# Moving the late DMA issues of a fused GFNet and FFN training kernel from SyncE's queue to GpSimd's, and some copies from ScalarE to VectorE

## The chip, the cores and the metric

The kernel runs on one core of one Trainium2 chip. The metric is the device time of that core in microseconds (us) for one execution of the whole program, which is a single launch. The kernel before takes 437.01 us, the median of three runs (436.89 to 438.28).

A core has engines with an instruction stream each: TensorE (matmuls; PE in the profile, with PEld for its weight loads), VectorE (DVE), ScalarE (ACT), GpSimd (POOL) and SyncE (SP), which only issues DMA transfers here. Every engine runs its stream in order, and waits at an instruction until the semaphores that it needs have come. A DMA transfer is issued by an engine's instruction, and then carried out by the DMA engines of the core while the issuing engine goes on.

## What is computed

The reference is one transformer-like block and all its gradients. Cut to what matters:

```python
def _fwd_reference(A_x, A_w_r, A_w_i, B_x, B_w1, B_b1, B_w2, B_b2, c, w_mod):
    def _A_ref(x, w_r, w_i):                       # GFNet filter
        X = rfft2(x.astype(float32), axes=(-2, -1))
        X = X * (w_r + 1j * w_i)
        return irfft2(X, s=(S, D)).astype(bfloat16)
    def _B_ref(x, w1, b1, w2, b2):                 # FFN with squared ReLU
        h = einsum('bsd,df->bsf', x, w1) + b1
        r = where(h > 0, h, 0)
        return einsum('bsf,fd->bsd', r * r, w2) + b2
    mod = (silu(c) @ w_mod).reshape(1, 6, 1, -1)
    sa, ca, ga, sb, cb, gb = (mod[:, i] for i in range(6))
    h = layernorm(x) * (1 + ca) + sa
    x = x + ga * _A_ref(h, w_r, w_i)
    h = layernorm(x) * (1 + cb) + sb
    return x + gb * _B_ref(h, w1, b1, w2, b2)

def reference(...):
    out, vjp = jax.vjp(f, A_x, A_w_r, A_w_i, B_w1, B_b1, B_w2, B_b2, c, w_mod)
    return (out, *vjp(grad_out))
```

x and grad_out are 1 x 2048 x 512, the FFN is 1792 wide, w_r and w_i are 2048 x 257, w_mod is 512 x 3072; all are bf16. There are ten outputs: the block's output and nine gradients.

## The kernel before

The Fourier transforms are matmuls with constant matrices, done in steps: f1 along the row, f2 and f3 across rows (both in the function `spec_f23`), and g1, g2, g3 back. The program goes through these phases:

1. Layer norm of x and f1; beside it, in the free time of TensorE, `ga = gT @ w2T` for all of the FFN's width. Then `spec_f23` with the filter's multiplication, and g1.
2. Per block of 512 rows: g2, g3, second norm, hidden layer, output layer, and the gradient back through the FFN's rows.
3. The spectrum window: `spec_f23` of the gradient, the gradients of w_r and w_i, and between its steps the gradient of w1 (`grad_w1`) and parts of the gradient of w_mod (`GMod.emit`).
4. The last window: g1, g2, g3 of the gradient, the first norm backwards in pairs of 128-row tiles (`row_pair`), and between them the gradient of w2 (`grad_w2`).

The code is written with a scheduler: `high_priority`, `Priority(tc, LATE)` and `issue_after` move instructions within an engine's stream. A tile pool with `bufs=n` gives n buffers in turn, and a tile waits until the last use of its buffer is over.

Phase 1. The scaling of w2T by `2 gb`, one half on VectorE and one on ScalarE, and the copies of ga out of PSUM, a third on VectorE:

```python
def scale_w2(h):
    for dc in range(4):
        wh = w2T[:, dc, h * F2:(h + 1) * F2]
        if h == 0:
            nc.vector.tensor_scalar(wh, wh, gb2x[:, dc:dc + 1], None, op0=ALU.mult)
        else:
            nc.scalar.activation(wh, wh, AF.Copy, scale=gb2x[:, dc:dc + 1])

for q in range(4):
    ...                                  # bn_stats of 4 tiles of x_sb, the last is `stats`
    if q == 1:
        with tc.issue_after(stats.ins): scale_w2(0)
    ...                                  # x_sb normalized, the last on ScalarE is `scaled`
    if q == 1:
        with tc.issue_after(scaled.ins): scale_w2(1)
    ...                                  # f1 of these tiles
nc.sync.dma_start(n1_dram, x_sb)         # 2 MB: the normalized rows, for the last window
...
nc.sync.dma_start(LF_dram, K["LFall"])   # a constant, later loaded transposed as LG
with Priority(tc, LATE):
    for b in range(NB):                  # 4
        for fc in range(NFC):            # 14
            ps = mmps.tile([P, SB], FP32, name="mm")
            for dc in range(4): nc.tensor.matmul(ps, lhsT=w2T[...], rhs=gT[b][:, :, dc, :], ...)
            with tc.high_priority():
                if fc % 3 == 0: nc.vector.tensor_copy(out=gaT[b][:, fc, :], in_=ps)
                else:           nc.scalar.copy(out=gaT[b][:, fc, :], in_=ps)
```

`spec_f23`, used in phases 1 (with `dc`, a constant term) and 3 (with `dc` None). After each of its eight f2 steps two strided halves of AE are copied out of PSUM, both by ScalarE:

```python
def spec_f23(tc, K, UT, AEs, dc, dest, elementwise, after):
    ...
    for gi in range(8):
        ...                              # f2: matmuls into ps
        nc.scalar.activation(dst[0], src[:, 0], AF.Copy, scale=EF_S)
        nc.scalar.activation(dst[1], src[:, 1], AF.Copy, scale=EF_S)
        if gi > 0: f3(gi - 1)            # matmuls, a copy, then elementwise(gi), after(gi)
# phase 1: the spectrum X in tiles Xs (memset on GpSimd), stored; parts of LG loaded transposed
def ew_f(gi, X):
    cmul(...)
    nc.sync.dma_start(xs_dram[:, gi], X)
    if 2 <= gi < 6: lg_part(gi - 2)      # LG <- LF_dram with transpose, LG_dram <- LG
```

Phase 2, its loads. `x1` is the first block of rows of x, for the second norm; w1T is loaded with a transpose:

```python
load_rows(0)                             # x1 <- x, on SyncE
nc.sync.dma_start(w1, w1_view)
nc.sync.dma_start(w2, w2_view)
nc.sync.dma_start(w1T, B_w1, transpose=True)
```

Phase 3. The gradient of w1 in 16 units of 16 matmuls, each evacuated by ScalarE into half of a tile of two buffers that a store empties:

```python
def grad_w1(fb, dc):
    ...                                  # 16 matmuls into ps
    if fb % 2 == 0: w1o[0] = gwa.tile([P, 2, W4], BF16, name="gw1", bufs=2)
    nc.scalar.copy(out=w1o[0][:, fb % 2, :], in_=ps[:, 0:W4])
    if fb % 2 == 1: nc.sync.dma_start(out4_view[...], w1o[0]...)

class GMod: def emit(self, jc, q, row, pool, ppool):
    ...                                  # gmbc: one row broadcast by a matmul
    for dc in range(0, 4, 2):
        wmc = pool.tile([P, 2, D], BF16, name="wmc", bufs=self.bufs)     # 2, later 4
        nc.sync.dma_start(wmc, self.wm_view[:, dc:dc + 2, cs])
        gwm = pool.tile([P, 2, D], BF16, name="gwm", bufs=self.bufs)
        for i in range(2): ...           # gwm = gmbc * scf; gsc = sum of wmc * gmbc
        nc.sync.dma_start(self.out9_view[:, dc:dc + 2, cs], gwm)

def load(gi): ...                        # SyncE: LF[gi] (gi >= 4), Z[gi], Xb[gi]
def ew_b(gi, G):
    cmul(...); cmul(...)                 # Z[gi] in place, and gW, a tile of 3 buffers
    for i, o in enumerate((out_2, out_3)):
        for p0_, n, rows_ in w_parts(o, gi):
            nc.sync.dma_start(rows_, gW[p0_:p0_ + n, i, :, 0:DF])        # 34 stores in all
def after_b(gi):
    if gi + 4 < 8: load(gi + 4)
    ...
    fill_w1(2 if 0 < gi < 6 else 1)      # units of grad_w1 in between
    if gi % 2 == 1: gms.pop(0)()         # one GMod.emit
```

Phase 4. `load_hn` is a transposing load; the row loads of pair t + 4 are issued after pair t:

```python
def load_hn():
    if fc < NFC:
        hns.append(endp.get("hn", gwp).tile([P, NT, P], BF16, name="hn", bufs=4))
        nc.sync.dma_start(hns[fc], h_dram[fc, :, :], transpose=True)

def grad_w2(fc):
    ...                                  # 16 matmuls of hns[fc] with g_sb
    nc.vector.tensor_tensor(gw, ps, modb[:, GB_B, :], op=ALU.mult)
    nc.sync.dma_start(out6_view[:, fc, :], gw)
    load_hn()

def load_rows3(t):
    if t < NT:
        rows3[t] = (fin.tile([P, 2, D], BF16, name="n1"), fin.tile([P, 2, D], BF16, name="gxl"))   # 2 buffers each
        nc.sync.dma_start(rows3[t][0], n1_dram[:, t:t + 2, :])
        nc.sync.dma_start(rows3[t][1], gx1_dram[:, t:t + 2, :])

def row_pair(t, Ts):
    n1, gxl = rows3[t]
    ...                                  # g3, copies out of PSUM, unfold: gh1
    nc.vector.tensor_tensor(gn, gh1, ..., op=ALU.mult)
    ...                                  # ScalarE: gs = gn * inv1
    nc.vector.tensor_tensor(q1, gh1, n1, op=ALU.mult)                      # L1231, the first use of n1
    ...
    for i in range(2):                                                     # L1239, the last use of n1
        nc.vector.tensor_scalar(gn[:, i, :], n1[:, i, :], rr[:, i, 3:4], rr[:, i, 2:3], op0=ALU.mult, op1=ALU.add)
    nc.vector.tensor_tensor(gs, gn, gs, op=ALU.add)
    nc.vector.tensor_tensor(gx, gs, gxl, op=ALU.add)
    nc.sync.dma_start(out1_view[:, t:t + 2, :], gx)
    load_rows3(t + 4)

nc.sync.dma_start(g_sb, g_view)
load_hn(); load_rows3(0); load_rows3(2)
for _ in range(3): load_hn()
...                                      # g1
for t in range(0, NT, 2):                # 8 pairs, with grad_w2 (fill) between them
    fill(1); row_pair(t, Ts); Ts = g2_pair(t + 2); ...
...                                      # the last two GMod.emit, the rest of grad_w2,
nc.sync.dma_start(out_8..., gcr)         # and the gradient of c
```

Of the kernel before, what the change touches and what calls it, by code (L numbers as in the profile page):

```python
# [9 lines left out]
AF = mybir.ActivationFunctionType  # L10
# [9 lines left out]
DF = 257  # L20
# [273 lines left out]
def spec_f23(tc, K, UT, AEs, dc, dest, elementwise, after=lambda gi: None):  # L294

    nc = tc.nc
    with tc.tile_pool(name="psB", bufs=1, space=PSUM) as psB_pool, \
# [14 lines left out]
        for gi in range(8):  # L312
# [12 lines left out]
            nc.scalar.activation(dst[1], src[:, 1], AF.Copy, scale=EF_S)  # L325
# [113 lines left out]
class GMod:  # L439
# [7 lines left out]
    def emit(self, jc, q, row, pool, ppool):  # L447
# [8 lines left out]
        for dc in range(0, 4, 2):  # L456
            wmc = pool.tile([P, 2, D], BF16, name="wmc", bufs=self.bufs)
            nc.sync.dma_start(wmc, self.wm_view[:, dc:dc + 2, cs])
# [8 lines left out]
            nc.sync.dma_start(self.out9_view[:, dc:dc + 2, cs], gwm)  # L467
# [3 lines left out]
def kernel(  # L471
# [144 lines left out]
    def scale_w2(h):  # L616
        for dc in range(4):
            wh = w2T[:, dc, h * F2:(h + 1) * F2]
            if h == 0:
                nc.vector.tensor_scalar(wh, wh, gb2x[:, dc:dc + 1], None, op0=ALU.mult)  # L620
            else:
                nc.scalar.activation(wh, wh, AF.Copy, scale=gb2x[:, dc:dc + 1])

    for q in range(4):
# [6 lines left out]
        if q == 1:  # L633
            with tc.issue_after(stats.ins):
                scale_w2(0)
# [4 lines left out]
        for j in range(4):  # L640
            t = 4 * q + j
            if j == 0:
                nc.vector.tensor_scalar(x_sb[:, t, :], x_sb[:, t, :], inv1[:, t:t + 1], nb[:, j:j + 1], op0=ALU.mult, op1=ALU.add)
            else:
                scaled = nc.scalar.activation(x_sb[:, t, :], x_sb[:, t, :], AF.Identity, bias=nb[:, j:j + 1], scale=inv1[:, t:t + 1])
        if q == 1:
            with tc.issue_after(scaled.ins):
                scale_w2(1)
# [40 lines left out]
    with Priority(tc, LATE):  # L689
        for b in range(NB):  # L690
            for fc in range(NFC):
# [3 lines left out]
                with tc.high_priority():  # L695
                    if fc % 3 == 0:
# [342 lines left out]
    def grad_b1():  # L1039
# [8 lines left out]
        nc.sync.dma_start(out_5.rearrange("(q f) -> q f", q=NFB), b4[0:P:32, :])  # L1048

    def add_quadrants(ps, pool, out, scale=None):  # L1050
# [6 lines left out]
        def add():  # L1057
# [7 lines left out]
            nc.sync.dma_start(out, row)  # L1065
# [11 lines left out]
    def grad_w1(fb, dc):  # L1077
# [8 lines left out]
        if fb % 2 == 1:  # L1086
            nc.sync.dma_start(out4_view[:, dc, (fb - 1) * W4:(fb + 1) * W4], w1o[0].rearrange("p a f -> p (a f)"))
# [16 lines left out]
    with tc.tile_pool(name="f23b", bufs=2) as fr, tc.tile_pool(name="ewb", bufs=2) as ew:  # L1104
# [12 lines left out]
        def ew_b(gi, G):  # L1117
# [3 lines left out]
            for i, o in enumerate((out_2, out_3)):  # L1121
                for p0_, n, rows_ in w_parts(o, gi):
                    nc.sync.dma_start(rows_, gW[p0_:p0_ + n, i, :, 0:DF])
# [23 lines left out]
    def grad_w2(fc):  # L1147
# [6 lines left out]
        nc.sync.dma_start(out6_view[:, fc, :], gw)  # L1154
# [12 lines left out]
    def load_rows3(t):  # L1167
        if t < NT:
            rows3[t] = (fin.tile([P, 2, D], BF16, name="n1"), fin.tile([P, 2, D], BF16, name="gxl"))
            nc.sync.dma_start(rows3[t][0], n1_dram[:, t:t + 2, :])  # L1170
            nc.sync.dma_start(rows3[t][1], gx1_dram[:, t:t + 2, :])
# [33 lines left out]
    with tc.tile_pool(name="psE", bufs=2, space=PSUM) as psE, tc.tile_pool(name="psS1", bufs=1, space=PSUM) as psS1:  # L1205
# [11 lines left out]
        def row_pair(t, Ts):  # L1217
# [25 lines left out]
            nc.sync.dma_start(out1_view[:, t:t + 2, :], gx)  # L1243
# [36 lines left out]
        nc.sync.dma_start(out_8.rearrange("b (dc p) -> (b dc) p", p=P), gcr)  # L1280
# [42 lines left out]
```

## Time and profile before

| | |
|---|---|
| time, median of 3 runs | 437.01 us (436.89 to 438.28) |
| span of the profiled execution | 436.5 us |
| granted TensorE clock, mean | 0.992 |
| DMA packets, bytes | 149,138 of 149,738 packets and 100.12 of 101.09 MB on the hardware queue of SyncE |
| costliest matmul groups | L694 58.1, L853 53.6, L1150 51.6, L1081 51.5, L880 49.9 and 49.1 us |

The stages, by the trace: the first phase without its spectrum pass runs to 57 us, the forward spectrum pass to 82, g1 to 92, rows and second norm until the first hidden-layer matmul (L853) at 116.8, the blocks of the FFN to 285, the spectrum window to 351, and the last window to the end.

How to read the lines. "L1231" is line 1231 of the kernel. A row of a timeline gives the start in us, the time from start to end, the engine, the line, the operation, the tiles as out<-in with their shape, and how many instructions the row joins; at its end, in brackets, the idle time before it and what ended that. In "[3.12 <-DMA n<-n_dram]" the engine stood idle for 3.12 us until the transfer into tile n landed. "SPq" is SyncE as an issuer of DMA: its time is that of the issue, not of the transfer. A "releaser" is found from semaphore events, and where an instruction waits for several things, the last to come is named.

Tile names in the profile are the program's, sometimes those of a reader or of an alias: n is `n1`, gw is both the tile `gw1` of `grad_w1` and the tile `gw` of `grad_w2` (the line tells which), gab is a block of `gaT`, and x is `x1` after 90 us.

### The profile page before, as it was taken

How to read it: one execution, taken by the hardware profiler on the slowest of the kernel's cores; microseconds unless marked ns; L12 is line 12 of the kernel's file. 1: busy time of each engine (PE TensorE's matmuls, PEld its weight loads, DVE VectorE, ACT ScalarE, POOL GpSimd, SP SyncE). 2: the span in 40 equal slices, each digit the busy share in tenths (PEclk: the TensorE clock that was granted, in tenths of full speed). 3: DMA queues.
4: the chain of work that ended last, by engine and by line, in shares of the span. 5: the costliest groups of instructions: out<-in, count | busy, mean ns of one | idle time of the engine just before them, and what ended most of it. 6: DMA issues, size and time to landing. Idle time of an engine off the chain costs nothing.

```text
span 436.5 us, 7027 instructions
## 1 busy us (share of the span) xinstructions
PE 398.5 (91%) x2353; PEld 195.4 (45%) x2375; DVE 351.4 (80%) x846; ACT 261.2 (60%) x493; POOL 13.0 (3%) x64
## 2 busy tenths in 40 slices
PE   2789989999999999999999999999899799993996
PEld 0335446654444434443444444455455464441332
DVE  6887758959997588969897998909686968978896
ACT  5797889769881286348536765365348375445331
POOL 6120000000000000000000000000000000000000
PEclk9998999999999999999999999999999999999899
DMA  8995779999298469669965997987995699999984
GB/s 240 238 291 146 188 290 267 279 311 256 91 379 245 136 114 352 165 165 229 270 195 153 222 338 267 211 204 229 273 300 158 168 253 259 222 260 244 275 235 144
DMA packets 149738, 101.09 MB, mean 232 GB/s; under 512 B 98753, under 2 KB 135494, under 8 KB 149062
## 3 DMA queue, kind: packets, MB, share of 16 engines
q1 hardware_dynamic: 149138, 100.12, 86.6%
q10 hardware_dynamic: 564, 0.53, 0.4%
q8 instruction: 18, 0.29, 0.3%
q14 instruction: 18, 0.15, 0.1%
HBM read 35.44 MB, written 41.60 MB: 176 GB/s over the span
## 4 chain that ended last, share of the span: by engine, by line
PE 35%; DVE 28%; DMA 14%; ACT 12%; SPq 5%; issue 5%; POOL 1%; ACTq 0%; DVEq 0%
PE og L880 10%; PE mm L853 6%; PE mm L694 4%; PE mm L1150 4%; DMA n<-n_dram 3%; DMA out_dram<-gw 2%; DMA x<-in_A_x_dram 2%; DVE gm_junk L465 2%; PE psG L341 2%; SPq L1145 2%; PE mod_ps L595 2%; PE mm L1081 2%; DMA n_dram<-x_sb 2%; DVE l_st L795 1%; ACT r L855 1%
## 5 line engine op out<-in xcount | busy, mean ns | idle before, releaser
L694 PE MATMUL mm<-gT,w2T 128*128 128x512 bf16 x224 | 58.1, 383 | 3.4 <-DVE gab L697 2.7
L853 PE MATMUL mm<-h2T,w 128*128 128x512 bf16 x224 | 53.6, 379 | 1.7 <-ACT r L855 1.5
L1150 PE MATMUL mm<-g_sb,hn 128*128 128x512 bf16 x217 | 51.6, 387 | 3.8 <-DVE gw L1153 3.4
L1081 PE MATMUL mm<-gab,h_sb 128*128 128x448 bf16 x256 | 51.5, 352 | 2.5 <-ACT gw L1085 2.5
L880 PE MATMUL og<-w1T,gab 128*128 128x512 bf16 x218 | 49.9, 379 | 1.1 <-DVE o L945 0.8
L880 PE MATMUL og<-w,h 128*128 128x512 bf16 x217 | 49.1, 379 | 0.3
L855 ACT ACTIVATE r<-mm,b1col 128x512 bf16<-128x512 f32 x56 | 37.0, 684 | 6.1 <-PE mm L853 3.7
L1081 PEld LDWEIGHTS <-h_sb 128*128 128x128 bf16 x256 | 24.6, 98 | 24.2 <-issue 3.6
L853 PEld LDWEIGHTS <-w 128*128 128x128 bf16 x224 | 21.1, 97 | 30.6 <-issue 8.8
L1150 PEld LDWEIGHTS <-hn 128*128 128x128 bf16 x224 | 21.3, 99 | 29.8 <-issue 7.1
L880 PEld LDWEIGHTS <-h 128*128 128x128 bf16 x224 | 21.8, 98 | 26.1 <-issue 0.9
L880 PEld LDWEIGHTS <-gab 128*128 128x128 bf16 x224 | 21.6, 98 | 25.9 <-issue 1.4
L694 PEld LDWEIGHTS <-w2T 128*128 128x128 bf16 x224 | 20.9, 98 | 23.1 <-issue 6.5
L893 ACT CAST G<-og 128x512 bf16<-128x512 f32 x16 | 9.2, 580 | 27.9 <-PE og L880 27.9
L699 ACT CAST gab<-mm 128x512 bf16<-128x512 f32 x36 | 21.7, 602 | 3.0 <-PE mm L694 2.9
L857 DVE TENSOR_TENSOR h<-r 128x1024 bf16<-128x1024 bf16 x28 | 19.2, 687 | 4.8 <-ACT r L855 4.8
L1085 ACT CAST gw<-mm 128x448 bf16<-128x448 f32 x16 | 8.7, 543 | 24.0 <-DMA out_dram<-gw 15.0
L1230 ACT ACTIVATE gs<-gn,inv 128x512 bf16<-128x512 bf16 x16 | 11.4, 716 | 18.3 <-DVE gn L1228 18.3
L413 DVE TENSOR_TENSOR p<-Z,G 128x1028 bf16<-128x1028 bf16 x8 | 5.6, 697 | 19.9 <-DMA Xb<-xs_dram 11.6
L372 ACT ACTIVATE Tsb<-psT 128x512 bf16<-128x512 f32 x32 | 18.5, 604 | 1.6 <-PE psT L370 1.6
L465 DVE SCALAR_TENSOR_TENSOR gm_junk<-wmc,onef,gmbc 128x512 bf16<-128x512 bf16 x24 | 17.9, 747 | 1.9 <-DMA wmc<-in_w_mod_dram 1.0
L697 DVE CAST gab<-mm 128x512 bf16<-128x512 f32 x20 | 13.7, 686 | 6.8 <-PE mm L694 6.7
(287 smaller groups left out, 757.1 us busy)
## 6 DMA issues: line engine op xcount, KB each, us to landing
h_dram<-h SPq DMA_DIRECT2D x28, 256.0 KB, 3.6
gh_dram<-gab SPq DMA_DIRECT2D x28, 256.0 KB, 3.8
w<-in_B_w_dram SPq DMA_DIRECT2D x2, 1792.0 KB, 7.7
wmc<-in_w_mod_dram SPq DMA_DIRECT2D x12, 256.0 KB, 4.7
out_dram<-gwm SPq DMA_DIRECT2D x12, 256.0 KB, 3.7
wz_dram<-Z SPq DMA_DIRECT2D x8, 258.0 KB, 2.4
xs_dram<-Xs SPq DMA_DIRECT2D x8, 258.0 KB, 3.2
Z<-wz_dram SPq DMA_DIRECT2D x8, 258.0 KB, 4.3
```

Of the source, the lines that this page charges most:

```text
L372: nc.scalar.activation(Tsb, ps, AF.Copy, scale=EF_S)
L465: nc.vector.scalar_tensor_tensor(out=junk, in0=wmc[:, i, :], scalar=K["onef"], in1=gmbc, op0=ALU.mult, op1=ALU.mult, accum_out=self.gsc[:, ...
L694: nc.tensor.matmul(ps, lhsT=w2T[:, dc, fc * P:(fc + 1) * P], rhs=gT[b][:, :, dc, :], start=(dc == 0), stop=(dc == 3))
L697: nc.vector.tensor_copy(out=gaT[b][:, fc, :], in_=ps)
L699: nc.scalar.copy(out=gaT[b][:, fc, :], in_=ps)
L853: nc.tensor.matmul(ps, lhsT=w1[:, dc, (fc + i) * P:(fc + i + 1) * P], rhs=h2T[b][:, :, dc, :], start=(dc == 0), stop=(dc == 3))
L855: nc.scalar.activation(r[:, i, :], ps, AF.Relu, bias=b1col[:, fc + i:fc + i + 1])
L857: nc.vector.tensor_tensor(h2, r, r, op=ALU.mult)
L880: nc.tensor.matmul(ps, lhsT=lhs(fc), rhs=rhs[:, fc, :], start=(fc == 0), stop=(fc == NFC - 1))
L1081: nc.tensor.matmul(ps[:, 0:W4], lhsT=h2_sb[:, t, dc * P:(dc + 1) * P], rhs=ghn[t // 4][:, t % 4, fs], start=(t == 0), stop=(t == NT - 1))
L1150: nc.tensor.matmul(ps, lhsT=hns[fc][:, t, :], rhs=g_sb[:, t, :], start=(t == 0), stop=(t == NT - 1))
L1230: nc.scalar.activation(gs[:, i, :], gn[:, i, :], AF.Copy, scale=inv1[:, t + i:t + i + 1], accum_out=rr[:, i, 0:1])
```

## The change

In phases 3 and 4 all transfers were issued by SyncE, among them the transposing loads, in the order of the program. The change leaves the transposes and the loads of the spectrum with SyncE, and moves the rest to GpSimd, which has hardly any work after the first phase: the stores of the gradients of w1, w2, w_r, w_i, w_mod, x, b1, b2 and c, the loads of w_mod's blocks (wmc) and the row loads (n1, gxl). A store that waits for its data then holds up no load behind it on SyncE, and a row load doesn't wait for a transpose to be issued.

In phase 1 it shifts work from ScalarE to VectorE: the second of the two AE copies in the forward `spec_f23`, the half of w2's scaling that ScalarE did, and half instead of a third of the ga copies. The scaling of w2 is also placed earlier in the stream.

```diff
@@ spec_f23
             nc.scalar.activation(dst[0], src[:, 0], AF.Copy, scale=EF_S)
-            nc.scalar.activation(dst[1], src[:, 1], AF.Copy, scale=EF_S)
+            if dc is None:
+                nc.scalar.activation(dst[1], src[:, 1], AF.Copy, scale=EF_S)
+            else:
+                nc.vector.tensor_scalar(dst[1], src[:, 1], EF_S, None, op0=ALU.mult)
@@ GMod.emit
-            nc.sync.dma_start(wmc, self.wm_view[:, dc:dc + 2, cs])
+            nc.gpsimd.dma_start(wmc, self.wm_view[:, dc:dc + 2, cs])
 ...
-            nc.sync.dma_start(self.out9_view[:, dc:dc + 2, cs], gwm)
+            nc.gpsimd.dma_start(self.out9_view[:, dc:dc + 2, cs], gwm)
@@ scale_w2
-            if h == 0:
-                nc.vector.tensor_scalar(wh, wh, gb2x[:, dc:dc + 1], None, op0=ALU.mult)
-            else:
-                nc.scalar.activation(wh, wh, AF.Copy, scale=gb2x[:, dc:dc + 1])
+            nc.vector.tensor_scalar(wh, wh, gb2x[:, dc:dc + 1], None, op0=ALU.mult)
+
+    scale_w2(0)
 ...
         if q == 1:
             with tc.issue_after(stats.ins):
-                scale_w2(0)
+                scale_w2(1)
 ...
-        if q == 1:
-            with tc.issue_after(scaled.ins):
-                scale_w2(1)
@@ ga copies
-                    if fc % 3 == 0:
+                    if fc % 2 == 0:
                         nc.vector.tensor_copy(out=gaT[b][:, fc, :], in_=ps)
@@ grad_b1, add_quadrants, grad_w1, ew_b, grad_w2, load_rows3, row_pair, end
-        nc.sync.dma_start(out_5.rearrange("(q f) -> q f", q=NFB), b4[0:P:32, :])
+        nc.gpsimd.dma_start(out_5.rearrange("(q f) -> q f", q=NFB), b4[0:P:32, :])
 ...
-            nc.sync.dma_start(out, row)
+            nc.gpsimd.dma_start(out, row)
 ...
-            nc.sync.dma_start(out4_view[:, dc, (fb - 1) * W4:(fb + 1) * W4], ...)
+            nc.gpsimd.dma_start(out4_view[:, dc, (fb - 1) * W4:(fb + 1) * W4], ...)
 ...
-                    nc.sync.dma_start(rows_, gW[p0_:p0_ + n, i, :, 0:DF])
+                    nc.gpsimd.dma_start(rows_, gW[p0_:p0_ + n, i, :, 0:DF])
 ...
-        nc.sync.dma_start(out6_view[:, fc, :], gw)
+        nc.gpsimd.dma_start(out6_view[:, fc, :], gw)
 ...
-            nc.sync.dma_start(rows3[t][0], n1_dram[:, t:t + 2, :])
-            nc.sync.dma_start(rows3[t][1], gx1_dram[:, t:t + 2, :])
+            nc.gpsimd.dma_start(rows3[t][0], n1_dram[:, t:t + 2, :])
+            nc.gpsimd.dma_start(rows3[t][1], gx1_dram[:, t:t + 2, :])
 ...
-            nc.sync.dma_start(out1_view[:, t:t + 2, :], gx)
+            nc.gpsimd.dma_start(out1_view[:, t:t + 2, :], gx)
 ...
-        nc.sync.dma_start(out_8.rearrange("b (dc p) -> (b dc) p", p=P), gcr)
+        nc.gpsimd.dma_start(out_8.rearrange("b (dc p) -> (b dc) p", p=P), gcr)
```

That is 107 issues of 34 gW, 12 wmc, 12 gwm, 8 + 14 gw, 8 n1, 8 gxl, 8 gx and 3 small ones. The scheduler, given the new program, also orders some of SyncE's instructions anew: the load of x1 stands behind the transposing load of w1T where it stood ahead of it, and the store of the constant LF stands behind the last transpose of gT.

## The prediction

> **What bounds the kernel now.** I read the busy shares first, then cut the span into its stages by windows, then read the timelines of SyncE's DMA queue, VectorE, ScalarE and TensorE in each stage.
>
> ```profile
> PE 398.5 (91%) x2353; PEld 195.4 (45%) x2375; DVE 351.4 (80%) x846; ACT 261.2 (60%) x493; POOL 13.0 (3%) x64
> ```
>
> TensorE (PE) is busy 91% of 436.5 us, so at most some 38 us are idle, and VectorE (DVE) is next. GpSimd (POOL) is free. The windows by stage (columns: length, busy us and count of PE, PEld, DVE, ACT, POOL, then granted clock, DMA share, GB/s):
>
> ```profile
> 57.00:82.00 25.00, 22.24 (x168) 13.68 (x167) 18.24 (x45) 23.26 (x43) 0.67 (x9) 1.00 1.06 298
> 285.00:351.00 66.00, 60.74 (x470) 35.62 (x469) 45.90 (x108) 33.49 (x62) 0.00 (x0) 1.00 0.75 223
> 351.00:436.50 85.50, 74.15 (x412) 33.74 (x417) 69.89 (x171) 38.45 (x82) 0.00 (x0) 0.98 0.96 236
> ```
>
> Outside the first microseconds, most of the idle TensorE time that one can hope for lies in the last window: 11.3 us, against 5.3 us in the spectrum window (285 to 351). In the first spectrum pass (57 to 82) ScalarE is busy 93% of the time. Now the queue of SyncE in the last window, where a transposing load holds the queue while it is issued:
>
> ```profile
> 351.20 7.23 SPq L1145 DMA_TRANSPOSE hn<-h_dram  x1
> 358.48 1.26 SPq L1170 DMA_DIRECT2D n<-n_dram  x1
> ...
> 383.73 4.86 SPq L1145 DMA_TRANSPOSE hn<-h_dram  x2
> 388.68 0.53 SPq L1170 DMA_DIRECT2D n<-n_dram  x1
> ...
> 393.27 4.46 SPq L1145 DMA_TRANSPOSE hn<-h_dram  x1
> 397.83 0.52 SPq L1170 DMA_DIRECT2D n<-n_dram  x1
> ```
>
> Each row load n is issued the moment the transposes before it are through. VectorE then waits for it, and TensorE waits for VectorE:
>
> ```profile
> 392.68 0.69 DVE L1231 TENSOR_TENSOR q<-gh,n 128x1024 bf16<-128x1024 bf16 x1 [3.12 <-DMA n<-n_dram]
> 401.80 0.69 DVE L1231 TENSOR_TENSOR q<-gh,n 128x1024 bf16<-128x1024 bf16 x1 [1.38 <-DMA n<-n_dram]
> ```
> ```profile
> 397.96 0.38 PE L1060 MATMUL mm<-b,ones_col 128*1 128x512 bf16 x1 [3.48 <-DVE gn L1239]
> 403.15 1.86 PE L1150 MATMUL mm<-g_sb,hn 128*128 128x512 bf16 x4 [3.40 <-DVE gw L1153]
> ```
>
> Those two holes in TensorE also cost clock: the windows from 395 to 415 us show 0.91 and 0.92 where the neighbours show 1.00. In the spectrum window the pattern is another one: ScalarE waits for the store of a weight gradient to free one of two buffers.
>
> ```profile
> 311.92 0.53 ACT L1085 CAST gw<-mm 128x448 bf16<-128x448 f32 x1 [7.96 <-DMA out_dram<-gw]
> 328.09 0.53 ACT L1085 CAST gw<-mm 128x448 bf16<-128x448 f32 x1 [7.05 <-DMA out_dram<-gw]
> ```
>
> **What the Trainium skill says.** (1) "DMA: Bandwidth & Descriptors", section "Issuing engines are not separate DMA queues": all queues feed the same 16 engines, so a second issuing engine saves issue time alone, usually small. The trace agrees on plain copies (0.35 to 0.6 us an issue here), not on transposes: 7.23 and 4.86 us of issue stand ahead of the row loads above, and that is what a second queue saves. (2) The same page, "Latency and other measured facts": about 1 us to the first byte from GpSimd's queue, with descriptors written in software, against 0.6 us from SyncE's. No run here shows GpSimd issuing a DMA. (3) "SBUF — State Buffer", "Who interferes with whom": VectorE copies and tensor_scalar in two-port modes and GpSimd exclude each other, each for a whole instruction; tensor_tensor does not stop descriptor writing (the page calls this inferred). No trace here shows it; the exposed operations in the last window are L1239 (16 x 0.41 us) and L464.
>
> **The change part by part.**
>
> *Step 1, first phase, engine time.* ScalarE loses four w2 scalings (4 x 1.04 us), 8 of 36 gab copies (8 x 0.60) and 8 AE copies (8 x about 0.8): 4.2 + 4.8 + 6.4 = 15.4 us. VectorE takes them: 4 x 0.45 + 8 x 0.69 + 8 x 0.69 (an evacuation of 128x512 from PSUM costs it 0.69) = 12.8 us. In the instruction order of the changed kernel, 184 of the 224 mm matmuls stand ahead of the g1 stage, against 144 before: 40 x 0.215 us = 8.6 us of TensorE work is meant to be done earlier.
>
> *Step 2, what gates the first phase.* That is not worth 8.6 us. The Xs tiles wait for the 2 MB store of x_sb to be read out: GpSimd's memset of Xs waits 6.5 us and ScalarE starts at 64.97 us, after SyncE has worked through its Z loads until 57.4 us. Neither moves. Then LG follows: the LF store, issued at 61.05 and landed 10.7 us later, is put behind the last transpose of gT in the new order, which I put at +1 to +2 us; issuing the last two LG transposes back to back returns about 0.6 us. And the order of SyncE changes here:
>
> ```profile
> 91.72 0.33 SPq L763 DMA_DIRECT2D x<-in_A_x_dram  x1
> 92.10 13.61 SPq L983 DMA_TRANSPOSE w1T<-in_B_w_dram  x1
> ```
>
> In the changed program x stands behind w1T. It landed at 101.5 us; now I expect 105 to 108. From landing to the first hidden-layer matmul it took 15.3 us (to 116.8), with VectorE full; without 4 gab copies of 0.6 us inside that stretch, and with the unfolding done while waiting, I put it at 9 to 12 us. So the hidden layer begins at 114 to 120, middle 117.3: **+0.5 us**. The middle of the kernel, 117 to 285 us, keeps its TensorE order and moves with its start.
>
> *Step 3, spectrum window.* 107 DMA issues move to GpSimd in all (34 gW, 12 wmc, 12 gwm, 8 + 14 gw, 8 n, 8 gxl, 8 gx, 3 small). 58 fall between about 299 and 350 us. Their order is static: the first gw store comes after 6 gW stores, the second 10 entries later. If one costs GpSimd about 1 us (an estimate: the page's first-byte figure taken as issue cost), the first goes out at 299 + 6 = 305 rather than 307.5, the second at 315 rather than 310.4, and the third near 320 rather than 322. The first and third gate the 7.96 and 7.05 us waits, behind which TensorE loses only 1.7 and 0.8 us; the second could become a new gate. Of the 5.3 us of holes I count on **-2 us**.
>
> *Step 4, last window.* Row loads no longer stand behind transposes. n for the fifth pair can be issued once L1239 of the third pair has run, at 381.1, not 388.68; it lands (3.95 to 4.2 us) before 389.5, where VectorE began to wait. VectorE's waits there are 1.7 (first n), 3.1, 1.4, 1.1 and about 1.4 in smaller ones: 8.7 us. VectorE becomes the bound of this window; its order is unchanged. I take 7 of the 8.7 as gained: **-7 us**.
>
> *Step 5, tail.* The last four stores (two gwm, one gw, gcr) go one after another through GpSimd. At 1 us against SyncE's 0.3 to 0.6, and with a slower first byte, I add **+1.5 us**.
>
> Sum: +0.5 - 2 - 7 + 1.5 = -7, so 430. I keep 1.5 us back for tensor_scalar against GpSimd, a quarter of a microsecond at 6 of the 16 places. **Predicted: 431.5 us.**
>
> **The rivals.**
> (a) *GpSimd's queue becomes the bound.* For it: 58 issues in 51 us, full at 0.9 us each. At 1.4 us they would take 81 us, the second gw store would leave 14 us late, and the first row loads, which stand behind all of them, would not leave before about 370. Then step 3 turns to +8 or more and step 4 shrinks to -3: 443 to 448 us. Against it: nothing in this trace, as POOL issued no DMA.
> (b) *The queue is no limit and the engines take it.* If a GpSimd issue costs what SyncE's does (0.6 us), the spectrum window loses nearly all its holes (-5) and the row loads leave at about 348: 423 to 426 us.
> (c) *The transfers were bound by the DMA engines anyway.* The DMA share in 355 to 385 us is 1.06 to 1.12. If transposes and row loads share rather than queue, each lasts longer, hn comes late in place of n, and step 4 gives only -2 or -3: 434 to 437.
> (d) *The first phase decides.* If x lands at 108 or later and its chain still takes 15 us, the hidden layer starts 6 us late and eats the gain: 437.
>
> **Range and chances.** (b) is the low side and (a) the high side; (c) and (d) lie between my number and no change. I give (b) 0.2, (a) 0.15, the middle the rest. Eight in ten: 422 to 443. 2% is 8.7 us, so faster by over 2% means below 428.3: 0.33. Slower means above 445.7: 0.14. Within: 0.53.
>
> **What would show it.** Right: the two waits for n at L1231 are gone, PE shows no hole over 1 us between 390 and 405, the clock there is 1.00; x lands after w1T but the first matmul of L853 stands within 3 us of 116.8; the first n leaves before 353. Wrong: POOL's DMA issues over 1.2 us on the mean, ScalarE's waits for out_dram<-gw growing, L1239 lengthened well over 0.41 us, or a TensorE hole of several us ahead of L853.

## The result, and the profile after

The changed kernel takes 444.17 us in the median against 437.49 of the kernel before: a ratio of 1.014, with a 95% interval of 1.0105 to 1.0175. It is slower by 1.4%; 431.5 us was predicted, and 444.17 lies outside the range of 422 to 443. The profiled execution spans 442.5 us, 6.0 more than before.

The page after, its busy shares and its DMA queues (columns of a queue: packets, MB, share of the 16 engines over the span):

```profile
PE 401.4 (91%) x2353; PEld 196.4 (44%) x2375; DVE 361.7 (82%) x866; ACT 250.7 (57%) x473; POOL 77.2 (17%) x171
...
q1 hardware_dynamic: 131328, 81.75, 71.0%
q0 software_dynamic: 6208, 18.37, 13.8%
```

18.37 MB have moved to GpSimd's queue (q0), and 10 us of work from ScalarE to VectorE. To see where 6 us went, four marks were read in both traces: the first matmul of the hidden layer, the first of the spectrum window, the last of g1, and the copy of gcr, the last computation. In the answers by tile, the two numbers ahead of the semicolon are the first and last start. Before:

```profile
L853 PE MATMUL mm<-h2T,w x224: 376/379/390, 116.8 to 254.2; 128*128 128x512 bf16 x112
L318 PE MATMUL psB<-Cdb,utcs x64: 216/219/230, 283.3 to 332.5; 128*128 128x128 bf16 x64
L341 PE MATMUL psG<-LGb,Z x64: 269/273/284, 340.8 to 353.4; 128*128 128x256 bf16 x64
L1279 DVE COPY gcr<-mm x1: 202/202/202, 433.5 to 433.5; 4x128 bf16<-4x128 bf16 x1
```

After:

```profile
L851 PE MATMUL mm<-h2T,w x224: 376/379/631, 121.7 to 259.5; 128*128 128x512 bf16 x112
L318 PE MATMUL psB<-Cdb,utcs x64: 216/219/230, 288.7 to 336.6; 128*128 128x128 bf16 x64
L344 PE MATMUL psG<-LGb,Z x64: 269/272/286, 344.9 to 356.0; 128*128 128x256 bf16 x64
L1277 DVE COPY gcr<-mm x1: 203/203/203, 438.4 to 438.4; 4x128 bf16<-4x128 bf16 x1
```

| stage | before | after | difference | predicted |
|---|---|---|---|---|
| until the hidden layer | 116.8 | 121.7 | +4.9 | +0.5 |
| FFN | 166.4 | 167.1 | +0.7 | 0 |
| spectrum window, g1 included | 70.2 | 67.3 | -2.9 | -2 |
| last window, until gcr | 80.3 | 82.6 | +2.3 | -7 |
| tail, gcr to the end | 2.8 | 3.9 | +1.1 | +1.5 |

So the spectrum window and the tail came out about as predicted. Two terms failed: the first phase, by 4.4 us, and the last window, by 9.3. Each of these numbers is one execution's. How far they scatter can be seen from the experiments. The last window took 77.6 to 81.8 us in the five kernels that leave it alone (before, e2, e3, e4, e9), and 82.6, 83.6 and 85.1 in the three with all of its queue change (after, e11, e1): it did not become 7 us shorter, and the +2.3 is about the size of the scatter. The hidden layer began at 115.4 to 118.2 us wherever the first phase was left alone, and at 119.3 to 122.8 wherever it was changed.

**The first phase.** Its spectrum pass reads from the copies of Xs, 65.0 to 81.8 us before (16.8), 66.6 to 87.4 after (20.8). Windows of 5 us over the pass (columns: length, busy us and count of PE, PEld, DVE, ACT, POOL, clock, DMA share, GB/s), before:

```profile
70.00:75.00 5.00, 4.55 (x41) 3.16 (x41) 4.41 (x10) 5.00 (x10) 0.00 (x0) 1.00 1.17 224
75.00:80.00 5.00, 4.71 (x40) 3.07 (x39) 4.50 (x10) 5.00 (x11) 0.00 (x0) 1.00 1.21 199
```

and after:

```profile
65.00:70.00 5.00, 4.92 (x44) 3.35 (x42) 5.00 (x21) 4.80 (x10) 0.67 (x9) 1.00 1.15 211
70.00:75.00 5.00, 4.27 (x36) 2.55 (x35) 5.00 (x12) 4.53 (x8) 0.00 (x0) 1.00 0.90 371
75.00:80.00 5.00, 4.87 (x38) 3.10 (x36) 5.00 (x11) 3.92 (x8) 0.00 (x0) 1.00 0.78 179
80.00:85.00 5.00, 5.00 (x43) 3.42 (x43) 5.00 (x12) 3.20 (x6) 0.00 (x0) 1.00 1.08 324
85.00:90.00 5.00, 4.93 (x34) 2.97 (x32) 5.00 (x11) 3.38 (x7) 0.00 (x0) 1.00 1.12 256
```

Before, ScalarE was full; after, VectorE is full for 25 us on end and ScalarE is not. The work was moved from one bound to another that is tighter: a step of the pass now costs VectorE two products (0.69 each), two sums (0.42), an AE half (0.73), and often a ga copy (0.68).

TensorE's clock went down with it. From 92 us to the hidden layer TensorE waits 5.7 us for ScalarE (0.5 before), and the clock is below full from 105 to 135 us, where the same two windows before show 1.00. After:

```profile
105.00:120.00 15.00, 9.19 (x62) 4.79 (x60) 13.48 (x35) 12.32 (x24) 0.00 (x0) 0.85 0.80 266
120.00:135.00 15.00, 14.27 (x60) 6.41 (x62) 13.57 (x30) 10.46 (x18) 0.00 (x0) 0.81 0.49 165
```

That is the 631 ns of the longest hidden-layer matmul above, against 390 before. It is not what made the hidden layer late: in e3 and e4 below, which are as late, the clock from 100 to 120 us is 1.00.

**The last window.** What TensorE waited for, in the list of waits (total us, times, longest), after:

```profile
PE mm L1148 <- DMA hn<-h_dram: 9.0, 3, 3.6
PE psG L344 <- DVE utcs L349: 0.5, 1, 0.5
PE mm L1275 <- DVE gcb L1273: 0.5, 1, 0.5
```

The waits for n are gone, as predicted, and 9.0 us of waits for hn, the transposed hidden layer, stand in their place. The queues from 351 to 390 us say why. First the sum of all, then each queue with packets, MB and share of the 16 engines, then the issues with the median us to landing. Before:

```profile
DMA packets 18111, 9.52 MB, mean 244 GB/s; under 512 B 16187, under 2 KB 16699, under 8 KB 17979
...
q1 hardware_dynamic: 18107, 9.47, 105.2%
...
n<-n_dram SPq DMA_DIRECT2D x5, 256.0 KB, 4.2
...
hn<-h_dram SPq DMA_TRANSPOSE x8, 7.9
```

After:

```profile
DMA packets 10598, 9.38 MB, mean 240 GB/s; under 512 B 9266, under 2 KB 9266, under 8 KB 10466
...
q1 hardware_dynamic: 9058, 4.35, 54.9%
q0 software_dynamic: 1536, 4.98, 50.0%
...
n<-n_dram POOLq DMA_DIRECT2D x5, 256.0 KB, 9.0
...
hn<-h_dram SPq DMA_TRANSPOSE x6, 12.7
```

In both kernels the 16 engines are full, and carry the same 9.4 to 9.5 MB at the same rate. (This is no fixed bound: in the runs below the same 39 us carried from 8.5 MB, in e6, to 10.4 MB, in e8 and e12.) What differs is who gets them. One queue served the transposes in SyncE's order; two queues take about half each, and GpSimd's half goes to row loads, stores and four wmc blocks that nobody needs before 420 us; the kernel before issues these four after 391 us. Eight transposes were issued in that stretch before, six after.

### The profile page after: what moved, and what is told of

Same layout as the page of the kernel before. It is cut to its first block, busy times and chain, and to the rows that moved or that the text cites. A ratio compares the mean times of both kernels' runs of the same rounds, so it can differ in the third digit from the quotient of the medians.

```text
span 442.5 us, 7078 instructions
## 1 busy us (share of the span) xinstructions
PE 401.4 (91%) x2353; PEld 196.4 (44%) x2375; DVE 361.7 (82%) x866; ACT 250.7 (57%) x473; POOL 77.2 (17%) x171
## 3 DMA queue, kind: packets, MB, share of 16 engines
q0 software_dynamic: 6208, 18.37, 13.8%
## 4 chain that ended last, share of the span: by engine, by line
DVE 35%; PE 32%; DMA 12%; SPq 8%; ACT 5%; issue 5%; POOL 2%; POOLq 0%; DVEq 0%; ACTq 0%
PE og L878 8%; PE mm L851 7%; PE mm L692 4%; SPq L1143 4%; DMA hn<-h_dram 4%; PE mm L1079 3%; PE mm L1148 2%; DVE gm_junk L468 2%; DMA w2T<-in_B_w_dram 2%; PE psG L344 2%; DVE gab L695 2%; DVE l_st L793 2%; SPq L566 2%; DVE p L417 2%; DVE p L416 1%
## 5 line engine op out<-in xcount | busy, mean ns | idle before, releaser
L692 PE MATMUL mm<-gT,w2T 128*128 128x512 bf16 x224 | 57.1, 388 | 3.7 <-DVE gab L695 2.8
L851 PE MATMUL mm<-h2T,w 128*128 128x512 bf16 x224 | 54.7, 387 | 1.3 <-ACT r L853 1.1
L1079 PEld LDWEIGHTS <-h_sb 128*128 128x128 bf16 x256 | 24.6, 98 | 22.8 <-issue 2.1
L695 DVE CAST gab<-mm 128x512 bf16<-128x512 f32 x28 | 19.2, 684 | 6.4 <-PE mm L692 6.2
L1121 POOL DMA_DIRECT2D out_dram<-gW x34 | 19.9, 608 | 22.2 <-issue 14.1
L697 ACT CAST gab<-mm 128x512 bf16<-128x512 f32 x28 | 16.5, 589 | 5.9 <-PE mm L692 5.7
```

The costliest lines, as they stand in the source:

```text
L692: nc.tensor.matmul(ps, lhsT=w2T[:, dc, fc * P:(fc + 1) * P], rhs=gT[b][:, :, dc, :], start=(dc == 0), stop=(dc == 3))
L851: nc.tensor.matmul(ps, lhsT=w1[:, dc, (fc + i) * P:(fc + i + 1) * P], rhs=h2T[b][:, :, dc, :], start=(dc == 0), stop=(dc == 3))
L1079: nc.tensor.matmul(ps[:, 0:W4], lhsT=h2_sb[:, t, dc * P:(dc + 1) * P], rhs=ghn[t // 4][:, t % 4, fs], start=(t == 0), stop=(t == NT - 1))
L1121: nc.gpsimd.dma_start(rows_, gW[p0_:p0_ + n, i, :, 0:DF])
```

## The experiments

Theory A, from these traces: the first phase loses by itself (VectorE bounds the pass, f1 is late), and the last window is bound by the bytes of 350 to 390 us, so that a second queue only chooses which transfer is late. Each group of runs had its own runs of the kernel before beside it (medians from 432.6 to 437.3 us), so the ratio is the measure. The table gives the stages as above, in us, each from one profiled execution; the FFN took 166.2 to 167.1 us in all of them. The ratios leave out executions of over 1.5% above the fastest of their kernel, seven of twenty in e7, and among them the profiled ones of e1 and e5, whose spans are 1.8 and 7.3 us above the longest of those kept: the stages of these two rows (*) carry no argument alone.

| run | ratio, 95% interval | hidden layer at | spectrum | last | tail | GpSimd issues |
|---|---|---|---|---|---|---|
| changed kernel | 1.0140 (1.0105 to 1.0175) | 121.7 | 67.3 | 82.6 | 3.9 | 107 |
| e1_queue * | 1.0154 (1.0113 to 1.0194) | 117.8 | 70.5 | 85.1 | 3.9 | 107 |
| e2_first | 1.0122 (1.0071 to 1.0173) | 122.1 | 68.5 | 77.6 | 2.8 | 0 |
| e3_scale | 1.0145 (1.0105 to 1.0184) | 122.7 | 68.8 | 81.8 | 2.8 | 0 |
| e4_copies | 1.0202 (1.0152 to 1.0253) | 122.8 | 69.9 | 78.8 | 2.8 | 0 |
| e5_wmc_sync * | 1.0200 (1.0164 to 1.0235) | 117.2 | 65.8 | 88.7 | 9.9 | 95 |
| e6_rows_sync | 1.0253 (1.0205 to 1.0301) | 115.4 | 66.5 | 86.3 | 9.6 | 91 |
| e7_rows_only | 1.0051 (1.0017 to 1.0085) | 115.9 | 67.9 | 81.7 | 2.9 | 16 |
| e8_stores_only | 1.0172 (1.0140 to 1.0204) | 116.9 | 65.8 | 81.6 | 8.6 | 79 |
| e9_window_stores | 0.9944 (0.9914 to 0.9974) | 117.8 | 66.6 | 80.3 | 2.6 | 51 |
| e10_no_gxl | 1.0215 (1.0154 to 1.0275) | 122.1 | 67.3 | 82.0 | 4.7 | 99 |
| e11_no_ae | 1.0241 (1.0175 to 1.0306) | 119.3 | 68.6 | 83.6 | 3.9 | 107 |
| e12_rows_act | 1.0107 (1.0055 to 1.0160) | 118.2 | 71.4 | 82.0 | 2.3 | 0 |
| e13_after_less | 1.0195 (1.0152 to 1.0237) | 122.2 | 68.7 | 76.3 | 9.6 | 91 |
| e14_before_less | 0.9881 (0.9816 to 0.9946) | 117.4 | 67.9 | 75.5 | 2.8 | 0 |
| e15_rows_early | 0.9943 (0.9921 to 0.9964) | 115.6 | 66.3 | 79.7 | 2.6 | 51 |
| e16_rows_early_sync | 1.0019 (0.9999 to 1.0039) | 116.6 | 71.5 | 77.7 | 2.8 | 0 |

### The two halves of the change: e1_queue, e2_first

```diff
 e1: nc.sync -> nc.gpsimd for the 107 late issues; w2 scaling, AE and ga copies as before
 e2: w2 scaling, AE and ga copies as in the change; all transfers on nc.sync
```

> The kernel before with only the GpSimd queue part of the change; the first phase is untouched. Theory A, two losses: the first phase costs 5 us by itself and the last window costs 3 us because row loads and transposes now share the DMA engines. Then the hidden layer starts at 116.8 as before, the spectrum window gives 2 to 3 us back, the last window is 2 to 6 us longer than before with holes of TensorE that wait for hn, and the time is 436 to 441 us. Rival B, one loss: the queue part gains what was predicted (7 us and more) once the first phase doesn't shift it, and the whole loss is the first phase's. Then 427 to 432 us.

> The kernel before with only the first-phase parts (w2 scaling, AE halves and half of the ga copies on VectorE); all transfers stay with SyncE. Theory A: the hidden layer starts 4 to 6 us late, nothing gives it back, 441 to 444 us. Rival B (the loss needs both parts, the first phase alone is neutral): 436 to 438 us.

Either half alone loses as much as the whole. e1's ratio of 1.0154 lies above both expectations; rival B, that the queue part gains once the first phase is left alone, falls. Theory A had the spectrum window give 2 to 3 us back, and the one profiled execution doesn't show it (70.5). In e2 the time is as theory A had it, and the hidden layer starts at 122.1, 5.3 us late, about as much as the 1.2% of its time. The two halves don't add up: together they cost no more than either. Why was not tried.

### Inside the first phase: e3_scale, e4_copies, e11_no_ae

```diff
 e3 (on before): scale_w2 all on nc.vector, scale_w2(0) ahead of the loop; AE and ga copies as before
 e4 (on before): AE halves to nc.vector, ga copies fc % 2; scale_w2 as before
 e11 (on after):
-            if dc is None: ... else: nc.vector.tensor_scalar(dst[1], src[:, 1], EF_S, None, op0=ALU.mult)
+            nc.scalar.activation(dst[1], src[:, 1], AF.Copy, scale=EF_S)
```

> The kernel before with only the w2 scaling changed (all on VectorE, the first half ahead of the norm's loop). Theory A1: the scaling waits for the transposing load of w2T in VectorE's stream, with the norm of the second four tiles and f1 behind it, so f1 runs about 5 us late and with it the hidden layer: 440 to 443 us. Rival A2: the lateness comes of the copies that VectorE takes over (AE, ga), and the scaling alone gives 436 to 438 us.

> The kernel before with only the copies moved (AE halves in the forward pass, ga copies half and half); the w2 scaling as before. In this order too the load of x stands behind the transposing load of w1T. Theory A1: f1 is on time, the late x costs 1 to 3 us, 437.5 to 440 us. Rival A2: the copies are the loss, 441 to 443 us.

> The changed kernel with the AE halves of the forward pass back on ScalarE. Theory A3, VectorE bounds that pass in the changed kernel (busy 5.00 of 5 us from 65 to 90 us, of which AE is 8 x 0.73): the pass from the first Xs to the last shortens by 2 to 4 us from 20.8, the hidden layer starts at 117.5 to 120 instead of 121.7, ratio 1.003 to 1.010. Rival A1, the late f1 alone sets it: the hidden layer still starts at 121 to 123, ratio 1.012 to 1.018.

Each part alone makes the hidden layer start 6 us late, for a different reason. In e3 the expected time came, but not for the expected reason: f1's last matmul is only 1.8 us later than before. VectorE waits for GpSimd in the middle of the pass:

```profile
67.30 0.87 DVE L152 TENSOR_SCALAR gen_v<-cf_dr,cf_f 128x128 int32<-128x128 int32 x4 [5.57 <-POOL cf_dr L141]
```

GpSimd's iota for a constant stands behind the memset of Xs in the new order, and that memset waits for the store of x_sb. So a part that touches neither moved an instruction of a third engine behind a gate. The changed kernel has that order too (its iota is at 66.49 us, before at 58.42), but VectorE has other work until then, so there it shows as 1.6 us of constants (L152 to L155) inside the full pass. In e4, f1 is on time, and the pass takes 22.8 us (Xs from 65.8 to 88.6). VectorE is full in it from 75 us on; ahead of that it waits 4.4 us for Xs, and TensorE's clock is 0.50 from 65 to 70 us. So the copies alone do cost what A2 said and more, but how much of it is VectorE's load and how much the clock isn't shown:

```profile
65.00:70.00 5.00, 2.56 (x16) 1.89 (x16) 2.87 (x6) 4.14 (x7) 0.42 (x8) 0.50 1.02 358
75.00:80.00 5.00, 5.00 (x43) 3.41 (x42) 5.00 (x12) 3.98 (x9) 0.00 (x0) 1.00 1.18 226
```

In e11 the stages answer to A3: the pass takes 18.9 us (67.5 to 86.4), just short of the 2 us less that A3 named, with ScalarE full again from 75 to 85 us and VectorE not, and the hidden layer starts at 119.3, 2.4 us sooner than in the changed kernel. Its time doesn't: a ratio of 1.0241 is above both expectations, so the gain of that stage was not found again in the total, and the case for A3 rests on the trace.

### Which transfers on which queue: e5_wmc_sync, e6_rows_sync, e7_rows_only, e8_stores_only, e12_rows_act

```diff
 e5: as e1, but wmc <- nc.sync          e6: as e1, but n1, gxl <- nc.sync
 e7: before, but n1, gxl <- nc.gpsimd   e8: before, but all stores -> nc.gpsimd
 e12: before, but n1, gxl <- nc.scalar
```

> The kernel before, late transfers on GpSimd's queue as in the change, but the loads of wmc stay with SyncE. Theory M1: from 351 to 390 us the DMA engines are full in both orders (9.5 MB at 240 to 244 GB/s); two queues share them half and half, so what GpSimd issues early takes its bytes from the transposes of hn, and TensorE waits for hn. Four loads of wmc (1 MB, not needed before 420 us) go behind the transposes again: about 4 us less of holes than with all on GpSimd (443.9), so 438 to 441 us. Rival M2: the crowding doesn't matter, GpSimd's queue or its instructions cost time by themselves (slow stores, disturbed VectorE): 442 to 445 us.

> As the change's queue part, but the row loads n1 and gxl stay with SyncE, between the transposes as before. M1: the row loads no longer compete with the transposes ahead of them, but the four wmc loads still do; VectorE's waits for n come back in part: 437 to 441 us. M2: 441 to 445 us.

> The kernel before with only the row loads n1 and gxl on GpSimd, all else on SyncE. M1: the waits for n are gone, but the first four row loads now share with g_sb and the first hn; holes for hn of 1 to 4 us: 434 to 439 us. M2 (few issues on GpSimd, so little cost): 430 to 434 us.

> The kernel before with only stores on GpSimd; wmc, n1 and gxl loads stay with SyncE. M1: stores go out when their data is there, loads keep their order; the spectrum window gives 1 to 3 us, the last window is as before within 2 us: 433 to 437 us. M2 (most of the 107 issues are on GpSimd): 441 to 444 us.

> The kernel before with only the row loads n1 and gxl issued, by ScalarE instead of SyncE. M1, any second queue takes its share from the transposes: like the same loads on GpSimd (ratio 1.005) within 0.006, with holes of TensorE at the same place. Rival M2, it is GpSimd's queue with software descriptors that does the harm: 0.985 to 0.997, the waits for n gone and none for hn or stores in their place.

Most of these numbers were missed, and the misses taught more than the hits. The times of e5, e6 and e8, taken as ratios, all lie above what either theory gave, and nearer to M2's. In e6 the window got worse, 86.3 us: one wait for hn is 8.4 us, VectorE waits 13.7 us for n again, and from 370 to 390 us the clock is 0.74. (e5's profiled execution, one of the two that carry nothing alone, shows 13.3 us of waits for hn, with the wmc loads ahead of the later transposes in SyncE's queue.) In e7 nothing waits for n or hn; VectorE waits for its own stores in their place:

```profile
DVE gx L1242 <- DMA out_dram<-gx: 4.5, 1, 4.5
DVE gw L1153 <- DMA out_dram<-gw: 4.0, 1, 4.0
```

Whatever stands behind in the crowd is late: hn, n, or the stores. That is the picture of a window bound by bytes, though in none of these runs was a size got right. In e12 the ratio is within 0.006 of e7's, as M1 had it, but not by M1's way: nothing waits for hn, which lands in 6.4 us in the median. ScalarE, which also computes, stops in its stream ahead of the issue of a row load (7.4 us in one case), and TensorE waits 8.0 us for ScalarE; the run doesn't tell whether GpSimd's queue is special.

e8 showed where the rest of the time went. Its stages are as M1 had them or better, and its end has a cost of GpSimd's queue, as M2 said, though not of the kind that it named. Its computation ends at 430.8 us, 2.9 us ahead of before, and the program ends 8.6 us after that, where before it took 2.8. SyncE at the end:

```profile
SPq L1318 <- DMA out_dram<-gcr: 16.7, 1, 16.7
SPq L1318 <- PEq L1318: 5.5, 2, 5.0
```

gcr has landed at 433.3 us, and then the last 5.0 us go to the closing barrier. The releaser is given as PEq, which had long been done; the trace's records show GpSimd in a drain instruction from 431.5 to 438.6. Such drains took 7.1 us with 79 issues (e8), 8.1 with 91 (e6, e13), 8.4 with 95 (e5), but 2.8 with 99 (e10) and 2.4 with the 107 of e1, e11 and the changed kernel. In these three with 107 GpSimd's stream has instead a gap of 4.1 us ahead of a store of gwm, at 427.8 us in the changed kernel, for which the trace names no wait. The tails of e5, e6 and e8 are 5.8 to 7.1 us longer than before, most of what their ratios lost. In e9 the drain (8.0 us) begins at 360.8 us, when GpSimd has issued its last store, and is over long before the end.

### Bytes or order in the last window: e10_no_gxl, e13_after_less, e14_before_less

```diff
 e10 (on after): gxl not loaded, gx = gs + n1 in place of gs + gxl
 e13 (on after), e14 (on before):
     def load_rows3(t):
+            if t >= 4:
+                rows3[t] = rows3[t % 4]; return
 and in GMod.emit, where self.bufs is 4: no load of wmc, gmbc in its place
```

All three leave work out: e10 half of the row loads, the others 12 of 16 row loads and four wmc blocks; so the gradient of x is not the reference's, and in e13 and e14 a part of that of c is made with another value.

> The changed kernel without the loads of gxl (8 of 256 KB; gx is made with n1 in place of gxl, so the gradient of x is not the reference's). M1, the last window is bound by what the DMA engines carry: about 1.3 MB less before 390 us, worth some 5 us at 240 GB/s; TensorE's waits for hn fall from 9.0 to 0 to 5 us and the window is 3 to 6 us shorter: ratio to before 1.000 to 1.008, against 1.014 of the changed kernel. Rival M3, transposes issued back to back limit each other whatever else runs: waits for hn stay at 8 us or more, ratio 1.011 to 1.017.

> The changed kernel with less to load in the last window: the row loads of the first two pairs are used for all eight (4 loads in place of 16), and the four late wmc loads are left out (gmbc stands in for wmc); 4 MB less in all, some 2 MB of it before 390 us. The gradients of x, w_mod's scale sums and c are not the reference's. M1, the DMA engines bound the window and the split between two queues chooses who waits: TensorE's waits for hn fall from 9.0 to under 3 us, the window from 82.6 to 72 to 78 us. M3, the transposes limit each other: waits for hn 6 us or more, window 80 us or more.

> The kernel before with the same loads left out. M1: the waits for n (6.2 us) and the two holes of TensorE (3.5 and 3.4 us) go with the loads, the window falls from 80.3 to 71 to 76 us, about as far as in the changed kernel with the same cut, so that without the crowding the queue makes little difference. Rival, the predicted reason (a row load that stands behind a transpose's issue): the loads being gone, the same 71 to 76 us, but the changed kernel with the cut is then no better than its 82 us less what the n loads cost.

e10 missed M1: waits for hn fell only from 9.0 to 7.2 us, the window by 0.6, and its ratio lies above both expectations. The fourth transpose still took 9.6 us of issue there. With nearly all of the other queue's loads gone, among them the four wmc blocks that leave from 365 to 373 us in the changed kernel, e13 answers: the waits of TensorE are down to

```profile
PE mm L1149 <- DMA hn<-h_dram: 2.6, 1, 2.6
PE psG L344 <- DVE utcs L349: 0.5, 1, 0.5
```

and the window to 76.3 us from 82.6. The transposes are again issued back to back, eight by 387.4 us. The first, beside g_sb and the first row loads, takes 9.9 us of issue as in the changed kernel (9.7); the seven after it take 1.9 to 5.3, where the fourth and fifth took 7.7 and 10.1 there. So it isn't the transposes that hold each other up, and M3 falls. With one queue and the same cut (e14) the window is 75.5. TensorE's share of the window is then whole:

```profile
351.00:390.00 39.00, 38.85 (x249) 19.14 (x248) 33.62 (x82) 22.31 (x50) 0.00 (x0) 1.00 1.06 247
```

Without the loads one queue is as good as two, within 0.8 us, and both windows are shorter than in any kernel with all of its loads (77.6 us and more). So in the changed kernel the loads of the other queue made hn late. That the waits for n before were the price of the same bytes is argued: they went with the loads in e14, as they would have by the predicted reason too. Nor do the bytes alone decide, as e10 shows. And a full share is no sign that somebody waits: in the line above it is still 1.06, at 247 GB/s, with ten transposes issued in place of eight. In e13's total time the gain doesn't show, as the drain (8.1 us) took it back.

### A version that beats both: e9_window_stores, e15_rows_early, e16_rows_early_sync

```diff
 e9 (on before): gW, gw1, b4 -> nc.gpsimd, and
+            (nc.gpsimd if self.bufs == 2 else nc.sync).dma_start(self.out9_view[:, dc:dc + 2, cs], gwm)
 e15 (on e9): pool fin allocated ahead of the spectrum window, and in after_b
+            if gi in (4, 5): load_rows3(2 * (gi - 4))
 e16: e15 with the stores of e9 back on nc.sync
```

> The kernel before with only the stores of the spectrum window on GpSimd (gW, gw1, b4, and gwm while it has two buffers); the last window is left as it was. Theory M1: stores leave SyncE's queue when the loads behind them matter and the DMA engines have room; the spectrum window loses 2 to 4.5 us, the last window stays at 80 us, and nothing is drained at the end: ratio to before 0.988 to 0.996. Rival M2 (GpSimd's queue is harmful anywhere): 1.00 to 1.01.

> The window-stores version (stores of the spectrum window on GpSimd, the rest on SyncE), and the row loads of the first two pairs issued by SyncE inside the spectrum window, after its fifth and sixth steps, 1 MB ahead of the crowded stretch. M1: the last window loses up to 4 us (1 MB at 240 GB/s) from 80.3, the spectrum window grows by less than 1.5: ratio to before 0.984 to 0.994. If the window were bound by issue order and not by bytes: no change against the window-stores version, 0.992 to 0.997.

> The kernel before with those early row loads alone, no transfer on GpSimd. M1: the last window loses up to 4 us, but the loads stand in SyncE's queue among stores that wait for their data, so the spectrum window may grow by 1 to 3 us: ratio 0.992 to 1.002.

e9 keeps of the change only what helped, and is faster than before, by 0.6%, as M1 had it: 0.9944 (0.9914 to 0.9974). The spectrum window takes 66.6 us, and ScalarE's list of waits there begins with

```profile
ACT gw L1085 <- PE mm L1081: 17.5, 10, 2.6
ACT utcs L348 <- PE psG L341: 5.0, 5, 2.6
```

where the kernel before had 15.0 us of waits for the store of gw. Moving 1 MB of row loads ahead (e15) adds nothing that can be measured (0.9943), and alone (e16) it is 1.0019: the last window is shorter by 2.6 us there, the spectrum window longer by 1.3, and a wait for n comes back at a later pair. M1 had up to 4 us less in e15's last window, which is 0.6 us shorter; the result is the one expected if issue order and not bytes bound the window. So what bounds the last window of the kernel before stays open between the two.

## Why the prediction was wrong, step by step

- **Step 1 (engine time) and step 2 (gates), the first phase.** Step 2 failed. It said that the gate of Xs decides, and put no cost on the work that VectorE takes over. The gate held within 1.6 us (66.6 against 65.0). But the 12.8 us which step 1 gave to VectorE (10.3 by the busy shares) were never laid against VectorE's load in the pass, 18.24 of 25 us in the window that the prediction itself shows. Eight AE halves (8 x 0.73 = 5.8 us), the ga copies and the late constants filled it, and the pass became 4.0 us longer. Gate and pass make 5.6 us, of which 4.9 reached the hidden layer. f1's last matmul, too, moved from 44.0 to 48.0 us, the scaling of w2 standing in VectorE's stream ahead of the norm with two waits of 1.0 us for w2T; what of this the gate felt isn't shown. The 8.6 us of TensorE work done sooner didn't help: it is the filler, and once used up, TensorE stood idle behind the chain from 110 us on. x landed at 108.4, as rival (d) had it, and VectorE waited only 1.3 us for it, as the chain was late already. The hidden layer began at 121.7, outside the 114 to 120 given.
- **Step 3, the spectrum window.** Right: -2.9 for -2, and for the reason given. ScalarE's waits for the store of gw fell from 15.0 to 9.2 us, and to nothing in e9; TensorE's waits fell from 5.2 to 2.5 us. One execution proves little here, but with the window's stores on SyncE and nothing else changed in it, it took 67.9 to 71.4 us in seven kernels (before, e2, e3, e4, e7, e12, e14), and with them on GpSimd 65.8 to 68.7 in all kernels but e1 (70.5). The issue of GpSimd was taken as 1 us, and was 0.61:

```profile
L1121 POOL DMA_DIRECT2D out_dram<-gW x34 | 19.9, 608 | 22.2 <-issue 14.1
```

- **Step 4, the last window.** This step failed, -7 us predicted and +2.3 measured, and with it the sign of the whole. "Row loads no longer stand behind transposes" came true, but "it lands (3.95 to 4.2 us)" did not: from GpSimd n took 9.0 us, and hn 12.7. The waits for n were read as waits for an issue alone; that the engines behind the queue were full, 1.06 to 1.12 of DMA share in the windows of rival (c), was not laid against the 4 us. A sign that was named for being right came true without the gain: TensorE has no hole from 390 to 405 us, but three of 2.2 to 3.6 us, for hn, from 366 to 388. That is rival (c), whose mechanism the changed kernel and e13 bear out, even to "hn comes late in place of n"; its size, still a gain of 2 to 3 us, was not.
- **Step 5, the tail.** Right in size for this kernel, +1.1 for +1.5, and partly by luck: the last two issues took 0.57 and 0.56 us and not 1, and behind them ran a drain of 2.4 us that the step doesn't have. What the runs with 79 to 95 issues showed, 6 us more, was foreseen nowhere.
- **The 1.5 us held back** for VectorE against GpSimd were not needed: L1239, now L1237, has a median of 407 ns in both, with a longest of 632 where it had 414.
- **Rivals (a) and (b).** At 0.55 to 0.75 us an issue GpSimd's queue is no bound, against (a), whose 443 to 448 us hold the measured time by chance: its step 3 of +8 was -2.9. (b) had the issue cost right, and nothing of the gain that it hung on it. (d) had x and the hidden layer right within 1.1 us, and the reason only in part: the chain took 13.3 us from x and not 15.

The Trainium skill, "DMA: Bandwidth & Descriptors", section "Issuing engines are not separate DMA queues", had the decisive sentence, that all queues feed the same 16 engines. The prediction cited it and then made an exception for transposes. The traces of the two kernels agree with the page and not with what the exception was to bring: 9.4 to 9.5 MB in 39 us, through one queue or two.

Left open: why the two halves of the change cost together what either costs alone; what bounds the last window of the kernel before, bytes or issue order (e13 and e14 against e10 and e15); why e11's total doesn't show what its stage shows; what the drain of GpSimd waits for, and why it is short with 99 and 107 issues. Whether a second queue other than GpSimd's would share with the transposes in the same way was tried (e12) and not answered.

## What to carry to other kernels

Before moving a transfer to another queue, look at the DMA share of the stretch in which it waits. At 1.05, here, a second queue gave no more bytes in the changed kernel, only another order, and the order that program and buffers had made in one queue was no worse; where the share had room (0.75) and a buffer waited for its store, in the spectrum window, the move paid. And work taken off a full engine must be laid against the load of the receiving engine in the same stage, not in the whole span.

## What the hardware showed beyond this

- An issue of 256 KB took GpSimd 0.55 to 0.75 us (means by group), against 0.42 to 0.56 for the same transfers on SyncE before.
- With both queues busy and the engines full, the shares were 54.9% for 4.35 MB of q1, mostly transposes, and 50.0% for 4.98 MB of q0.
- The issue of a transposing load of hn, 512 KB each, took from 1.4 to 10.1 us in the changed kernel; the fourth and fifth took 7.7 and 10.1, and 3.2 and 1.9 in e13, without most of the other queue's loads.
- After 51 to 95 issues, GpSimd's last drain took 6.8 to 8.4 us, after 16 (e7) 4.3, after 99 and 107 2.4 to 2.8. In e9, where it began at 360.8 us, it cost nothing; where it began at the program's end (e5, e6, e8, e13), the tail grew from 2.8 to between 8.6 and 9.9 us.
- TensorE's clock was below full where it had holes: 0.74 from 390 to 410 us in e8, with a hole of 5.3 us, 0.74 from 370 to 390 us in e6, with one of 8.4, and 0.91 from 390 to 410 us before, with two of 3.5 and 3.4.
